# Routing batches of the last seven token tiles, the gate tiles, and the preparation of the output weights in a fused FFT and mixture-of-experts kernel

## The chip, the cores and the metric

One core of a Trainium2 chip. The metric is the device time of one execution in microseconds (us). A core has four compute engines with a queue of instructions each: TensorE (PE, matrix multiplication into PSUM banks), VectorE (DVE), ScalarE (ACT) and GpSimd (POOL). SyncE (SP) issues plain DMA transfers. POOL issues the indirect ones, those that gather or scatter rows by a list of indices. An instruction waits at the head of its engine's queue for semaphores, and everything behind it waits with it.

## What is computed

```python
X = np.fft.fft(np.fft.fft(x, axis=1), axis=2).real      # x: 8 x 3072 x 256
t = X.reshape(8 * 3072, 256)
h = np.maximum(np.maximum(t @ w1, t @ w2), t @ w3)       # 768 wide
x = h @ w_out                                            # 24576 tokens x 256
do = x @ w_skip > 0                                      # tokens that see an expert
e = argmax(x[do] @ w_gate)                               # one of 8 experts, F = 1024
y = softmax_gate * (np.maximum(x[do] @ e1[e], 0) @ e2[e])
out = x;  out[do] = x[do] + y
```

## The kernel before

The real part of the transform is symmetric, so the work is done on half spectra, and fp32 products are made of two or three fp32r products (a value's high part and the rest). Four phases follow each other.

1. The transform (`fft_phase`), with the weights of layer 1 (`prep_weights`) folded into the second transform.
2. The first expert network, on 25 tiles (`tiles`: 23 of 512 columns, then 256 and 264). `period(t)` works through 12 units of layer 1 of tile t: 6 blocks f of the hidden width, two halves i each. PE writes two banks "pa" and "pb" per unit (L484 to L488), DVE joins them (`even` L500, `minus` L503, `plus` L506, `peak` L514), ACT and POOL split the result into high part and rest (`ht`, L520 and L521). Between the units stand the pieces of layer 2 of tile t-1: `linear` (PE into bank pl, ACT copies to `lin` L553, POOL adds L556 and L558) and `rest` (PE pz L565, DVE zt L569). Tiles 0 and 1 are ordered by an automatic scheduler, the later ones as the code is written.
3. Routing, mixed into the same periods. The finished tokens of a batch of tiles (`BATCHES`) get scores, an expert and a place. `ship` stores tokens and copies ten gate columns into a tile `st` (ACT, L590). `finish` is a chain of small DVE steps (L598 to L624, with an ACT exponential L603). `place` counts the tokens ahead of each one (PE L634 and L636, then DVE up to the index list rI, L646). Then one `scatter` (POOL, L651) for each block of 128 tokens, 193 in all, writes token number and gate into the list `lst`, sorted by expert. `st` comes from a pool and is cleared on POOL (L921) at the first tile of a batch. The scatters wait in a Python list (`posted`), and `period` takes one out at each unit.
4. The second expert network, 256 tokens of one expert at a time. Three static steps, whose tokens are known early (from tile 18 on), stand in the program: `wide1` (PE, L785), `wide1_rest` (ACT, then DVE hs L789), `layer2_of` (PE pys, L798), `result` (DVE L802) and `place_rows` (POOL, L805). `table` (DVE, L841 to L876) works out for the remaining tokens which step takes which expert. It needs all counts and so the placing of the last tile. Its result `tab` lets SP load the first lists of tokens (ida, idn, idm) and the first weights (ws), and POOL gather the first tokens (Gd, L1139). Two dynamic loops follow.

Between tile 24 and the dynamic loops lies a tail. It holds layer 2 of tile 24, the routing of the last batches, all scatters not yet issued (`post`, with a tiny add `idle` on POOL between two of them), and the three static steps.

In phase 2, at tile 0, a generator (`prep_out`, L381 to L406) also prepares the output weights: for each block f a transposition (PE pT, ACT woT), a gate product (PE pg, ACT wof) and a product with w3 (PE pc), which collects in two of the five "pa"/"pb" banks.

## Time and profile before

| | |
|---|---|
| three timed runs | 1717.25, 1718.05, 1723.55 us (median 1718.05) |
| the profiled execution | 1719.05 us, of which the span of instructions is 1717.1 us |
| mean granted clock of PE | 0.977 of full speed |
| busy in the span | PE 1614.2 us (94%), DVE 1336.0 (78%), POOL 1121.5 (65%), ACT 739.0 (43%) |
| transform | up to about 178 us |
| tile 0 of the first network | PE from 188.15 us |
| layer 2 of tile 24 on PE (tail begins) | 1166.04 us |
| dynamic loops on PE begin | 1247.87 us |

All times within a trace count from the start of its span. What an engine waited for stands in brackets behind a row. Idle time counts only on an engine that sets the pace.

### The profile page before, as it was taken

To read this page: it belongs to the slowest core of one execution; us is meant where nothing else is said; L and a number is where in the kernel's file an instruction comes from. 1 tells how busy PE (TensorE), PEld (TensorE's weight loads), DVE (VectorE), ACT (ScalarE), POOL (GpSimd) and SP (SyncE) were. 2 spreads that over 40 slices of the span, in tenths; PEclk is the share of its full clock that TensorE was granted. 3 is DMA by queue.
4 is the path that set the end of the run, shared out by engine and by line. 5 is a ranking of instruction groups with operands and counts; after the bars stand their busy time and mean duration, and the time that the engine had idled before them with its cause. 6 is when DMAs were issued, how large, how long until landed. Compare 5 with 4: busy or idle time off the path is not lost. (4 is left out here: it accounts for less than half of the span.)

```text
span 1717.1 us, 33375 instructions
## 1 busy us (share of the span) xinstructions
PE 1614.2 (94%) x10837; PEld 1448.1 (84%) x10837; DVE 1336.0 (78%) x2288; ACT 739.0 (43%) x1437; POOL 1121.5 (65%) x1358
## 2 busy tenths in 40 slices
PE   6999699999999999999999999994799999999985
PEld 2565489989889989899898898984799999999975
DVE  7999488888788888888887878882477777777754
ACT  4555343333333333333333333331266666666654
POOL 2000355668878789789688788698456666676753
PEclk9999799999999999999999999997899999999998
DMA  8875420412211111111122111122266766766766
GB/s 324 306 281 205 151 61 32 129 44 48 59 44 44 44 44 44 50 50 44 57 44 59 47 44 41 42 51 71 69 218 223 229 218 220 231 220 220 232 197 214
DMA packets 109435, 212.47 MB, mean 124 GB/s; under 512 B 28107, under 2 KB 61292, under 8 KB 106228
## 3 DMA queue, kind: packets, MB, share of 16 engines
q1 hardware_dynamic: 94360, 188.65, 34.7%
q0 software_dynamic: 14112, 21.77, 4.1%
q8 instruction: 56, 0.92, 0.3%
q10 hardware_dynamic: 864, 0.79, 0.1%
q14 instruction: 43, 0.35, 0.1%
HBM read 157.82 MB, written 55.17 MB: 124 GB/s over the span
## 5 line engine op out<-in xcount | busy, mean ns | idle before, releaser
L565 PE MATMUL pz<-wo,ht 128*128 128x266 f32 x3474 | 484.2, 286 | 3.1 <-ACT lin L553 3.1
L565 PEld LDWEIGHTS pz<-wo,ht 128*128 128x128 f32 x3474 | 462.6, 189 | 21.7 <-ACT lin L553 3.4
L521 POOL TENSOR_TENSOR ht<-u,ht 128x512 fp32r<-128x512 f32 (+2 forms) x300 | 374.9, 1256 | 161.6 <-ACT ht L520 153.9
L520 ACT ACTIVATE ht<-u 128x512 fp32r<-128x512 f32 (+2 forms) x300 | 175.6, 610 | 308.8 <-DVE u L514 304.0
L651 POOL DMA_INDIRECT lst<-pair,rI x193 | 191.6, 993 | 35.4 <-issue 28.8
L785 PE MATMUL acc<-xd,wd 128*128 128x256 f32 x1632 | 193.6, 278 | 0.9 <-DVEq L1249 0.9
L785 PEld LDWEIGHTS acc<-xd,wd 128*128 128x128 f32 x1632 | 190.3, 188 | 1.2 <-issue 1.2
L829 DVE TENSOR_TENSOR wd<-ws,wd 128x1024 fp32r<-128x1024 f32 x150 | 177.6, 1225 | 16.2 <-issue 6.0
L828 ACT ACTIVATE wd<-ws 128x1024 fp32r<-128x1024 f32 x150 | 154.9, 1061 | 76.2 <-issue 46.5
L553 ACT ACTIVATE lin<-pl 128x266 f32<-128x266 f32 x194 | 75.0, 393 | 211.8 <-DVE zt L569 149.4
L500 DVE SCALAR_TENSOR_TENSOR u<-yb,wv,pa 128x512 f32<-128x512 f32 (+2 forms) x124 | 89.8, 724 | 93.2 <-PE pa L486 80.9
L484 PE MATMUL pa<-y,wt 128*128 128x512 f32 (+2 forms) x300 | 118.4, 395 | 13.3 <-DVE y L459 10.4
L503 DVE TENSOR_TENSOR pa<-r,pb 128x512 f32<-128x512 f32 (+2 forms) x150 | 100.4, 669 | 34.7 <-ACT r L498 32.6
L798 PE MATMUL pys<-wd,hs 128*128 128x256 f32 x960 | 125.5, 286 | 1.2 <-DVE hs L1196 0.9
L789 DVE SCALAR_TENSOR_TENSOR hs<-acc,hs 128x512 fp32r<-128x512 f32 x148 | 98.0, 687 | 29.0 <-ACT hs L786 24.3
L798 PEld LDWEIGHTS pys<-wd,hs 128*128 128x128 f32 x960 | 117.7, 190 | 2.3 <-DVE hs L1196 1.3
L786 ACT ACTIVATE hs<-acc 128x512 fp32r<-128x512 f32 x148 | 86.9, 599 | 75.5 <-PE acc L785 72.5
L484 PE MATMUL pb<-y,wt 128*128 128x512 f32 (+2 forms) x300 | 117.6, 392 | 0.0
L485 PE MATMUL pb<-y,wt 128*128 128x512 f32 (+2 forms) x300 | 117.3, 391 | 0.0
L485 PE MATMUL pa<-y,wt 128*128 128x512 f32 (+2 forms) x300 | 117.0, 390 | 0.0
L486 PE MATMUL pa<-y,wt 128*128 128x512 f32 (+2 forms) x300 | 116.7, 389 | 0.0
L486 PE MATMUL pb<-y,wt 128*128 128x512 f32 (+2 forms) x300 | 116.4, 388 | 0.0
(286 smaller groups left out, 3190.4 us busy)
## 6 DMA issues: line engine op xcount, KB each, us to landing
ws<-e SPq DMA_DIRECT2D x164, 512.0 KB
xt<-xf SPq DMA_DIRECT2D x24, 1024.0 KB
out<-zt SPq DMA_DIRECT2D x48, 512.0 KB
yr<-ysc SPq DMA_DIRECT2D x25, 512.0 KB
ysc<-ytc SPq DMA_DIRECT2D x8, 768.0 KB
yb<-yfsc SPq DMA_DIRECT2D x23, 256.0 KB
ysc<-yts SPq DMA_DIRECT2D x8, 672.0 KB
wr<-wm SPq DMA_DIRECT2D x6, 768.0 KB
```

The source lines that it names most:

```text
L484: nc.tensor.matmul(pt[:, :w], wt[f][:, g, 0, c], hi, start=True, stop=False)
L485: nc.tensor.matmul(pt[:, :w], wt[f][:, g, 0, c], lo, start=False, stop=False)
L486: nc.tensor.matmul(pt[:, :w], wt[f][:, g, 1, c], hi, start=False, stop=not whole)
L503: nc.vector.tensor_tensor(minus_to, r, pb[:, :w], ALU.subtract)
L520: nc.scalar.activation(ht[:, 0, :w], h[:, s, :w], AF.Copy)
L521: nc.gpsimd.tensor_tensor(ht[:, 1, :w], h[:, s, :w], bits(ht[:, 0, :w]), ALU.subtract)
L565: nc.tensor.matmul(pz[:, :SW], hs[s][f][:, g, c * P : c * P + P], wo[:, v, f], start=f == 0 and g == 0 and v == 0, stop=f == NC6 - 1 and g ...
L651: ins = nc.gpsimd.indirect_dma_start(out=lst[:, :], out_offset=bass.IndirectOffsetOnAxis(ap=ix[:, b : b + 1], axis=0), in_=pair[:, first + b],
L785: nc.tensor.matmul(ph[:, f % 2 * 256 : f % 2 * 256 + 256], lhs, rhs, start=n == 0, stop=n == 5)
L798: nc.tensor.matmul(py[:, :D], lhs, rhs, start=n == 0, stop=n == 23)
L828: nc.scalar.activation(hi, r, AF.Copy)
L829: nc.vector.tensor_tensor(lo, r, bits(hi), ALU.subtract)
```

## The change

- **Batches.** Before: seven batches of three tiles, then (21, 22), (23) and (24). Now: six of three, (18, 19), then every tile from 20 to 24 by itself. The index lists rI have four buffers and not two. From tile 20 on every third unit takes two scatters from the list, the second behind an `idle` add.
- **Gate tiles.** Two lasting tiles `st0` and `st1` are cleared once, and the batches take turns. L921 has gone from POOL's queue.
- **Layer 2 from tile 21 on.** The second ACT copy of `linear` is dropped, and DVE makes the additions straight from the PSUM bank, in POOL's place.
- **Output weights.** `prep_out` runs in three stages (`turn`, `gates`, `product`) that work on three neighbouring blocks at a time. Its sums and its one shared transposition bank lie in the three layer-2 banks ("pz"), no longer in "pa" and "pb".
- **Tail.** Seven and four steps of routing go ahead of the first two parts of the first static `wide1`, `table` comes right after them, and the first loads and the first gather of the dynamic steps are issued ahead of the results of static step 2. Gd has its own buffer.

```diff
-BATCHES = [(3 * k, 3 * k + 1, 3 * k + 2) for k in range(7)] + [(21, 22), (23,), (24,)]
+BATCHES = [(3 * k, 3 * k + 1, 3 * k + 2) for k in range(6)] + [(18, 19)] + [(t,) for t in range(20, 25)]
-F1, F2, F3 = 3, 5, 6
+F1, F2, F4 = 3, 5, (4, 7)
+TL = 21
+TP = 20
@@ prep_out
-    pc = [mp.tile([P, 512], F32, tag=tag, name="pc", bufs=n) for tag, n in (("pa", PA), ("pb", 5 - PA))]
-    for f in range(NC6):
-        wof, w3t = raw[f // 2][:, f % 2, 0], raw[f // 2][:, f % 2, 1]
-        wo = pool.tile([P, SW], F32, tag="ws", name="wof", bufs=2)
-        nc.scalar.activation(wo[:, :D], wof, AF.Copy)
-        wT = pool.tile([P, 2, P], F32, tag="ws", name="woT", bufs=2)
-        pt = mq.tile([P, 512], F32, tag="pz", name="pT")
...
+    *pc, pt = (mq.tile([P, 512], F32, tag="pz", name=nm) for nm in ("pc", "pc", "pT"))
+    def turn(f):
+        wof, _ = part(f)
+        ws[f] = pool.tile([P, 3, SW], F32, tag="ws", name="wof", bufs=2)
         for kt in range(2):
             nc.tensor.transpose(pt[:, kt * P : kt * P + P], wof[:, kt * P : kt * P + P], ident)
+        nc.scalar.activation(ws[f][:, 1, :D], pt[:, : 2 * P], AF.Copy)
+        nc.scalar.activation(ws[f][:, 0, :D], wof, AF.Copy)
+    def gates(f):
+        pg = pt[:, 2 * P : 2 * P + 10]
         for kt in range(2):
+            nc.tensor.matmul(pg, ws[f][:, 1, kt * P : kt * P + P], gs[:, kt], start=kt == 0, stop=kt == 1)
+        nc.scalar.activation(ws[f][:, 0, D:], pg, AF.Copy)
+    def product(f):
+        nc.scalar.activation(wo_t[:, 0, f], wo, AF.Copy)
         for g in range(2):
             nc.tensor.matmul(pc[g][:, :SW], w3t[:, g * P : g * P + P], wo, start=f == 0, stop=f == NC6 - 1)
         nc.gpsimd.tensor_tensor(wo_t[:, 1, f], wo, bits(wo_t[:, 0, f]), ALU.subtract)
+    for k in range(NC6 + 2):
+        for stage, f in ((gates, k - 1), (product, k - 2), (turn, k)):
+            if 0 <= f < NC6:
+                stage(f)
         yield
@@ linear
-                    nc.scalar.activation(lin[c][:, k], pl[:, :SW], AF.Copy)
+                    if k == 0 or t < TL:
+                        nc.scalar.activation(lin[c][:, k], pl[:, :SW], AF.Copy)
-                nc.gpsimd.tensor_tensor(lin[c][:, 2], lin[c][:, 0], lin[c][:, 1], ALU.add)
+                eng, odd = (nc.gpsimd, lin[c][:, 1]) if t < TL else (nc.vector, pl[:, :SW])
+                eng.tensor_tensor(lin[c][:, 2], lin[c][:, 0], odd, ALU.add)
@@ place
-            ix = mr.tile([P, KB], I32, tag="rI", name="rI")[:, :nb]
+            ix = mr.tile([P, KB], I32, tag="rI", name="rI", bufs=4)[:, :nb]
@@ arrive
-                stage["st"], stage["o"] = mr.tile([P, KB, 10], F32, tag="st", name="st"), 0
-                nc.gpsimd.memset(stage["st"][:, :, E1:], 1e-9)
+                stage["st"], stage["o"] = stage["sts"][k % 2], 0
@@ period
-                        if posted and (n < 9 or t + 1 < len(tiles)):
-                            posted.pop(0)()
-                if t == 0 and i == 1:
-                    for _ in range((0, 0, 1, 2, 2, 2)[f]):
-                        next(prep)
+                        for k in range(2 if t >= TP and n % 3 == 0 else 1):
+                            if posted and (n < 9 or t + 1 < len(tiles)):
+                                if k:
+                                    apart()
+                                posted.pop(0)()
+                if t == 0 and n >= 3:
+                    next(prep)
@@ tail
-            for _ in range(2):
-                fill()
-            for q in range(4):
+            for q in range(2):
+                for _ in range(F4[q]):
+                    fill()
                 wide1(x, w, h, q, ph[q])
-            for q in range(4):
-                for _ in range(F3):
-                    fill()
+            wide1_rest(h, 0, ph[0])
+            settle()
+            wide1_rest(h, 1, ph[1])
+            steps = table()
+            next(steps)
+            for q in range(2, 4):
+                wide1(x, w, h, q, ph[q])
+            for q in range(2, 4):
                 wide1_rest(h, q, ph[q])
-            settle()
```

**Order, PE at tile 0, in the middle of the output weights.** `pT` or `pg`, `pc` and `wof` belong to the preparation, `pa` and `pb` to layer 1. Before:

```order
L393 MATMUL pg<-gs,woT 128x10 x2
L389 MATMUL pT<-ident,wraw_1466 128x128 x2
L396 MATMUL pc<-wof,wraw_1466 128x266 x2
L484 MATMUL pb<-y_1358,wt_72 128x512
L485 MATMUL pb<-y_1358,wt_72 128x512
L486 MATMUL pb<-y_1358,wt_72 128x512
L393 MATMUL pg<-gs,woT 128x10 x2
```

Now, at the same unit (L498 to L500 are the old L484 to L486):

```order
L398 MATMUL pT<-gs,wof 128x10 x2
L406 MATMUL pc<-wof,wraw_1440 128x266 x2
L498 MATMUL pa<-y_1360,wt_72 128x512
L391 MATMUL pT<-ident,wraw_1442 128x128 x2
L499 MATMUL pa<-y_1360,wt_72 128x512
L500 MATMUL pa<-y_1360,wt_72 128x512
L498 MATMUL pb<-y_1360,wt_72 128x512
L499 MATMUL pb<-y_1360,wt_72 128x512
L500 MATMUL pb<-y_1360,wt_72 128x512
L398 MATMUL pT<-gs,wof 128x10 x2
```

The w3 product `pc` of a block used to stand one transposition behind the gate product of its own block. Now it stands a whole step, a unit of layer 1 or so, behind it.

**Order, POOL in the tail, from the scatters to the first dynamic gather.** `lst` scatters are those of the routing, `out<-Gs` those of static results. Before (of the tail's 34 scatters 29 stand ahead of the memset and five behind it):

```order
L651 DMA lst<-pair,rI 228480x2
L921 MEMSET st 128x24
L1032 TENSOR_TENSOR idle<-zz 128x2
L651 DMA lst<-pair,rI 228480x2
...
L805 DMA out<-Gs,ids_11716 27776x256
L1032 TENSOR_TENSOR idle<-zz 128x2
L1139 DMA Gd<-out,ida 128x256 x2
```

Now (all 16 scatters of the tail stand ahead of the results):

```order
L667 DMA lst<-pair,rI 228480x2
L751 TENSOR_TENSOR idle<-zz 128x2
L827 DMA out<-Gs,ids_11249 27776x256
L751 TENSOR_TENSOR idle<-zz 128x2
L827 DMA out<-Gs,ids_11249 27776x256
L751 TENSOR_TENSOR idle<-zz 128x2
L1137 DMA Gd<-out,ida 128x256 x2
L751 TENSOR_TENSOR idle<-zz 128x2
L827 DMA out<-Gs,ids_11260 27776x256
```

The memset has gone, 18 scatters have moved into the periods ahead, and the gather Gd stands ahead of the results of static step 2.

**Order, PE in the tail, from layer 2 of tile 24 on.** `pr` is the placing of tile 24, the `pc` product begins `table`, `pt` ends it. Before:

```order
L565 MATMUL pz<-wo,ht 128x266 x54
L785 MATMUL acc<-xs,wx 128x256 x48
L634 LDWEIGHTS tri
L634 MATMUL pr<-sl,tri 128x45
...
L798 MATMUL pys<-wx,hs 128x256 x24
L768 MATMUL acc<-ident,Gs 128x128 x4
L841 LDWEIGHTS ones
L841 MATMUL pc<-sl,ones 128x8
L798 MATMUL pys<-wx,hs 128x256 x24
L785 MATMUL acc<-xs,wx 128x256 x36
L875 MATMUL pt<-ident,r_12993 1x128 x2
```

Now:

```order
L581 MATMUL pz<-wo,ht 128x266 x54
L807 MATMUL acc<-xs,wx 128x256 x24
L650 LDWEIGHTS tri
L650 MATMUL pr<-sl,tri 128x45
...
L863 LDWEIGHTS ones
L863 MATMUL pc<-sl,ones 128x8
L807 MATMUL acc<-xs,wx 128x256 x24
L820 MATMUL pys<-wx,hs 128x256 x24
L897 MATMUL pt<-ident,r_12931 1x128 x2
L790 MATMUL acc<-ident,Gs 128x128 x4
```

The placing of tile 24 and the first product of `table` now stand between the two halves of the first `wide1`, and the end of `table` behind the first `layer2_of`.

## Rows read from the trace of the kernel before

**Rows 1.** Page, busy time of the engines over the span

```profile
PE 1614.2 (94%) x10837; PEld 1448.1 (84%) x10837; DVE 1336.0 (78%) x2288; ACT 739.0 (43%) x1437; POOL 1121.5 (65%) x1358
```

**Rows 2.** Windows: stretch, length, PE, PEld, DVE, ACT, POOL, PEclk, DMA share, GB/s

```profile
206.60:216.40 9.80, 9.64 (x27) 7.23 (x28) 3.10 (x5) 4.30 (x12) 7.85 (x7) 0.51 0.18 55
...
1110.00:1160.00 50.00, 46.67 (x380) 45.26 (x379) 38.97 (x112) 17.85 (x54) 44.42 (x55) 1.00 0.20 44
...
1172.80:1247.90 75.10, 41.98 (x312) 40.57 (x310) 24.14 (x65) 11.54 (x21) 46.87 (x78) 0.75 0.19 52
```

**Rows 3.** Timeline of PE in the tail: start, length, operation, wait in brackets

```profile
1172.82 5.81 PE L785 MATMUL acc<-xs,wx 128*128 128x256 f32 x48
1187.88 0.20 PE L634 MATMUL pr<-sl,tri 128*128 128x45 bf16 x1 [9.25 <-DVE sl L615]
...
1208.65 3.78 PE L798 MATMUL pys<-wx,hs 128*128 128x256 f32 x16 [18.24 <-DVE hs L789]
...
1221.64 2.89 PE L798 MATMUL pys<-wx,hs 128*128 128x256 f32 x24
1224.37 0.60 PE L768 MATMUL acc<-ident,Gs 128*128 128x128 f32 x4
...
1239.99 0.46 PE L768 MATMUL acc<-ident,Gd 128*128 128x128 f32 x2 [4.01 <-DMA Gd<-out,ida]
...
1247.87 2.30 PE L785 MATMUL acc<-xd,wd 128*128 128x256 f32 x16 [0.89 <-DVEq L1249]
```

**Rows 4.** Timeline of DVE in the tail

```profile
1181.35 0.17 DVE L646 CAST rI<-rs 128x4 int32<-128x4 f32 x1 [12.30 <-DMA lst<-pair,rI]
...
1184.80 0.20 DVE L598 TENSOR_REDUCE rm<-st 128x5 f32<-128x40 f32 x1 [0.28 <-ACT st L590]
...
1207.61 0.20 DVE L622 TENSOR_REDUCE rS<-st 128x5 f32<-128x45 f32 x1 [18.90 <-POOL st L921]
...
1214.45 0.16 DVE L843 TENSOR_TENSOR tf<-pc,kt 128x8 f32<-128x8 f32 x1
...
1218.29 0.15 DVE L871 TENSOR_SCALAR r<-r 128x1 f32<-128x1 f32 x1
```

**Rows 5.** Timeline of POOL in the tail

```profile
1207.42 0.15 POOL L921 MEMSET st<- 128x24 f32 x1
...
1211.03 0.99 POOL L651 DMA_INDIRECT lst<-pair,rI  x1 [3.33 <-DVE rI L646]
...
1216.55 0.99 POOL L651 DMA_INDIRECT lst<-pair,rI  x1 [0.16 <-issue]
...
1236.06 2.03 POOL L1139 DMA_INDIRECT Gd<-out,ida  x1 [6.24 <-issue]
```

**Rows 6.** Timeline of SP in the tail, the loads behind `tab`

```profile
1222.95 0.40 SPq L824 DMA_DIRECT2D ida<-lst  x1
```

**Rows 7.** Groups by line from 1060 to 1160 us: count, busy, mean ns

```profile
L651 POOL DMA_INDIRECT lst<-pair,rI x15 | 14.8, 990 | 2.4 <-issue 2.4
...
L556 POOL TENSOR_TENSOR lin<-lin 128x266 f32<-128x266 f32 x11 | 7.2, 659 | 0.1
```

**Rows 8.** The same view, DVE

```profile
L569 DVE TENSOR_TENSOR zt<-pz,lin 128x266 f32<-128x266 f32 x21 | 9.0, 429 | 0.6 <-issue 0.6
```

**Rows 9.** Timeline of PE at tile 0

```profile
206.68 2.14 PE L396 MATMUL pc<-wof,wraw 128*128 128x266 f32 x4 [2.81 <-ACT wof L394]
...
221.68 0.61 PE L393 MATMUL pg<-gs,woT 128*128 128x10 f32 x4 [0.61 <-ACT woT L390]
```

**Rows 10.** Timeline of ACT at tile 0

```profile
205.50 1.06 ACT L462 ACTIVATE y<-yr 128x1024 fp32r<-128x1024 f32 x1 [3.33 <-POOL yr L448]
```

**Rows 11.** Timeline of DVE at tile 0

```profile
214.94 0.75 DVE L500 SCALAR_TENSOR_TENSOR u<-yb,wv,pa 128x512 f32<-128x512 f32 x1 [6.66 <-PE pa L486]
...
223.38 0.75 DVE L500 SCALAR_TENSOR_TENSOR u<-yb,wv,pa 128x512 f32<-128x512 f32 x1 [2.49 <-PE pa L486]
...
234.97 0.68 DVE L514 SCALAR_TENSOR_TENSOR u<-u,pb 128x512 f32<-128x512 f32 x1
```

78 lines of the change are left out of this document (39 added, 39 removed).

## The prediction

> **What bounds the kernel now.** I read the page first. PE is busy for 94% of the span [rows 1], so the kernel is as fast as PE is kept fed, and what can be gained lies where PE stands. Windows show where that is. Inside the first network PE has next to no gaps. At tile 0 PE looks busy in 9.64 of 9.80 us, but the granted clock is 0.51, the 1.2 GHz level. In the tail PE is busy for 42 of 75.1 us, at a mean granted clock of 0.75 [rows 2]; more exactly it lasts 75.05 us, from the first `wide1` at 1172.82 to the dynamic loops at 1247.87 [rows 3].
>
> The timelines tell what PE stands for in the tail. It waits 9.25 us for `sl`, the last step of tile 24's routing that PE needs, then 18.24 us for `hs` [rows 3]. DVE explains both. It stood 12.30 us at the rI of tile 23, because that buffer was still read by a scatter; tile 24's outputs and routing were queued behind it. Then it stood 18.90 us at rS, waiting for the memset of `st`, and the `hs` that PE wanted was behind that [rows 4]. The memset lay on POOL at 1207.42, behind 29 scatters that follow one another every 1.38 us ((1216.55 - 1211.03) / 4) [rows 5]. So the chain is: scatters on POOL, memset, DVE, PE. `table` (1214.45 to 1218.44 on DVE [rows 4]), the load of ida (1222.95 [rows 6]) and the gather Gd (1236.06 [rows 5]) come after, and PE waits for Gd 4.01 us more [rows 3].
>
> **The tail.** With four rI buffers, the index list of tile 24 goes into that of tile 20, whose scatters are long done. With lasting gate tiles no memset stands behind scatters. Both DVE stalls lose their cause. What is left to PE is its own work, at full clock: three `wide1` of 48 matmuls (5.81 us each), six `layer2_of` of 24 (2.89 us each), three transpositions (0.60 us each) [rows 3], together 17.4 + 17.3 + 1.8 = 36.5 us, and about 1 us for placing and table products: 37.5.
>
> Then the new waits. All routing of tile 24 stands ahead of PE's third part of `wide1`. Layer 2 of tile 24 ends at 1172.82, and its last outputs on DVE a little later. From rm to the `sl` for PE took 3.1 us (1184.80 to 1187.88 [rows 3, 4]), so `sl` is ready at about 1176, when PE has just done the first half of `wide1` (2.9 us). PE places (0.4 us) and does the other half, to about 1179.2. DVE then has rI, two `hs` and the 4.0 us of `table` before it comes to the `hs` that `layer2_of` wants, at about 1181.5. I put 2.3 us for that, 0.9 for the loop's entry as before [rows 3], and 1 for small delays. So 37.5 + 4.2 = 41.7 us in place of 75.05: **33.4 us gained**.
>
> Is something else late? Of 34 scatters in the tail 16 remain, some 22 us from the start of the tail at 1166, to 1188. `tab` is ready at about 1185, so SP loads ida at about 1188, now behind the first weights. Before, Gd began 13.1 us after the load of ida (1222.95 to 1236.06 [rows 5, 6]). If it takes as long again, it begins at about 1201 and is there 4 us later (1236.06 to 1239.99 [rows 3, 5]), at 1205. PE needs it 4.4 us before the loop (a transposition, a `layer2_of` and the entry), at about 1210. It is covered by 5 us. The ends: 28 us if this chain or `table` sets the pace for some 5 us, 37 us if no new wait shows.
>
> **The last three tiles.** 18 scatters move into them. With the adds between, POOL gets 18 x 1.38 = 25 us more there at the most. It loses 25 additions in all, 20 of them inside the periods, at 0.66 us: 13 us [rows 7]. From 1110 to 1160 POOL is already busy for 44.42 of 50 us and PE only 46.67 [rows 2], so POOL can be full there for some microseconds. Full POOL means late `ht`, and PE's `pz` behind it. DVE gets the 20 additions, at the nearest row (zt, also from PSUM, 0.43 us [rows 8]) 8.6 us, and some 4 us for two more rounds of routing of 13 small steps. In the same stretch it is busy for 38.97 us of 50 [rows 2]; the half of those 12.6 us that falls into it brings it to 45. Both engines come close to PE's own pace without clearly passing it. I take a loss of 1.5 us; bounds are a gain of 1 (PE loses 3.3 of these 50 us today, and part of it can be waits that go) and a loss of 6 (POOL full, with half of its net 12 us turned into waits).
>
> A moved scatter ran beside an idle DVE in the tail and now runs beside a busy one. The 15 scatters between 1060 and 1160, beside a busy DVE, took 990 ns on average [rows 7], those of the tail 0.99 [rows 5]: no stretching. The Trainium skill, "SBUF — State Buffer", section "Who interferes with whom", says that VectorE and GpSimd share a pair of ports under an exclusive lock. By that rule each of the 18 scatters could stand behind one DVE operation of 0.43 us [rows 8], which makes POOL 8 us later, and at the same half the loss here would be 4 us more. The scatters' durations don't agree with it.
>
> **Tile 0.** Before, PE stood 2.81 us for `wof` [rows 9]. ACT had it ready to do, but stood itself at `y` of a later tile for 3.33 us [rows 10]. The clock then dropped, and `pc` held two of the five banks of layer 1, so DVE, which is the slowest here, ran dry: 6.66 and 2.49 us [rows 11]. From 208.28 (where the first of these waits begins) to the last `peak`'s end at 235.65 DVE has three blocks of eight operations of about 0.6 us, and two for `cc`: 15.6 us of work in 27.4. So 11.8 us is the most that can be gained. In three stages `pc` no longer waits for the `wof` just made, and layer 1 has all of its five banks. The `y` stays in ACT's queue, ahead of the next gate copy, but PE then has a unit of layer 1 to do, six matmuls: I let half of the 3.33 us come back, 1.7. The one transposition bank also ties PE to ACT once a step; over six steps I put 0.6 us each, as `pg` once waited for `woT` [rows 9], 3.6 in all. 11.8 - 1.7 - 3.6 gives **6.5 us gained**. Bounds: nothing (the waits take it all) and 11.
>
> **Costs at nothing.** The dropped ACT copies (ACT is busy for 43% [rows 1]) and `idle` adds in the periods are hidden behind PE.
>
> **Sum.** 1719.05 (this execution's own time, 1.0 above the median of the three runs) - 33.4 - 6.5 + 1.5 = 1680.7. The median of runs then is 1679.7; I say 1679.
>
> **Rivals.**
> - **The tail keeps half of its stall.** The chain of `table`, ida, Gd or the scatters is longer than I think: for example when Gd again waits for weights or results in flight. For it: 13.1 us passed from ida to Gd before, with nothing in between that the profile names (the bracket says "issue" [rows 5]). Against: it has 5 us to spare and no PE instruction waits for the scatters. If it lasts twice as long, 26 us, PE stands 8 us more; with `table` late too, 15. Time 1688 to 1695. Chance 0.13.
> - **POOL or DVE is the bound in the last tiles.** Loss of 6 to 10 us in place of 1.5: 1684 to 1688. For it: 44.42 of 50 us busy. Chance 0.14.
> - **Nothing from tile 0.** ACT and the single bank replace the waits, or the clock falls anyway: 1686. Chance 0.12.
> - **Slower than before.** The clock. PE's granted clock is 0.75 in the tail because it fell while PE stood. If PE's short waits are enough to keep it at 1.2 GHz, PE's 37.5 us in the tail become 75, with the waits 79 (+4). At tile 0 the 17.6 us of those 27.4 that lie outside the half-clock window take up to twice as long; I put half of that, 9 us. Time 1719 + 4 + 9 = 1732. It decides only from nine tenths of the tail's work at the low level on (37.5 x 1.9 + 4.2 = 75.5, the old time). Against: PE ran at 1.2 GHz only behind stalls of 2.81 us or more here [rows 2, 3, 9], and the one I expect is shorter. Chance 0.02. By the Trainium skill, "TensorE: Matmul & The Clock Gate", PE's clock follows its activity, which agrees with these rows.
>
> **Numbers.** My forecast has 0.55 (1672 to 1684); 0.04 is left for no change, where the moved scatters or `st` wait somewhere that I don't see and the tail's gain is lost. Range 1667 (tail 37, tile 0 11, median offset 1, and 3 of other small gains) to 1695 (half of the tail's stall kept, or two of the losses together). A change of less than 0.5%, 8.6 us, is about what a measurement of this kernel can't tell from none. Faster by more than that 0.94, within it 0.04, slower 0.02.
>
> **What would show it.** Right: no wait of DVE for `st` or for rI; PE from the first `wide1` to the loop in 40 to 44 us with a clock near 1.0; PE waiting some 2 us for `hs` behind `table`; Gd without a wait of PE; at tile 0 no stretch at half clock behind `pc`, and the first `pz` near 231 us and not 237.6. Wrong: a new wait of over 5 us in the tail (Gd, `tab`), `pz <- ht` or `pl <- lin` waits from 1060 us on, or a first `pz` after 235 us.

## The result

The changed kernel takes 1703.38 us (median of four runs, 1702.47 to 1704.85); the kernel before, run beside it, 1717.65 us (1714.57 to 1723.55). The ratio is 0.9914 with a 95% interval of 0.9886 to 0.9941: faster by 0.86%. The forecast was 1679 us, and 1703 lies above its range. The direction was right; of the 38.4 us forecast for the profiled execution 16.0 came (1719.05 to 1703.05).

The profile page of the changed kernel, busy time of the engines [rows 1]:

```profile
PE 1618.0 (95%) x10839; PEld 1452.9 (85%) x10839; DVE 1356.6 (80%) x2341; ACT 735.9 (43%) x1426; POOL 1115.1 (66%) x1321
```

PE is busy for 3.8 us more than before. A change that only takes waits away leaves PE's busy time alone or, with the clock back up, lowers it. So somewhere PE's own work has become slower. I divide the execution at three places on PE: the first `pz` (end of tile 0), the first static `wide1`, and the first dynamic step. Their starts in the changed kernel, in the timeline of PE:

```profile
231.36 1.86 PE L581 MATMUL pz<-wo,ht 128*128 128x266 f32 x13
...
1174.37 3.04 PE L807 MATMUL acc<-xs,wx 128*128 128x256 f32 x24
...
1180.38 1.58 PE L820 MATMUL pys<-wx,hs 128*128 128x256 f32 x12
1182.71 0.50 PE L820 MATMUL pys<-wx,hs 128*128 128x256 f32 x2 [0.75 <-issue]
1185.41 1.22 PE L820 MATMUL pys<-wx,hs 128*128 128x256 f32 x4 [2.20 <-DVE r L892]
1190.61 1.95 PE L820 MATMUL pys<-wx,hs 128*128 128x256 f32 x6 [3.98 <-ACT hs L808]
...
1193.49 3.98 PE L820 MATMUL pys<-wx,hs 128*128 128x256 f32 x24
...
1221.99 0.78 PE L807 MATMUL acc<-xd,wd 128*128 128x256 f32 x3 [0.88 <-DVEq L1273]
```

Before, the last two stood at 1172.82 and 1247.87 [rows 3], the span ended at 1717.1, and the first `pz` was

```profile
237.60 3.86 PE L565 MATMUL pz<-wo,ht 128*128 128x266 f32 x30
```

That gives a ledger (us, worked out from these starts and the ends of the spans):

```
                                 before    after   change  forecast
start to first pz (tile 0)       237.60   231.36    -6.2     -6.5
first pz to first wide1          935.22   943.01    +7.8     +1.5
first wide1 to dynamic loops      75.05    47.62   -27.4    -33.4
dynamic loops to the end         469.2    479.1     +9.9      0
sum                                                -16.0    -38.4
```

Three lines are off, and the largest miss is one that the prediction has no term for. The windows of the four places [rows 2] (columns: stretch, length, busy time and count of PE, PEld, DVE, ACT, POOL, granted clock, DMA share, GB/s):

```profile
206.60:216.40 9.80, 9.13 (x50) 7.79 (x51) 6.83 (x11) 6.93 (x20) 8.47 (x8) 1.00 0.17 55
1015.60:1061.83 46.23, 41.40 (x256) 36.27 (x254) 41.09 (x80) 13.93 (x30) 34.90 (x35) 1.00 0.13 38
1061.83:1174.37 112.54, 106.49 (x798) 100.56 (x799) 102.01 (x255) 33.35 (x85) 91.59 (x105) 0.98 0.24 63
...
1185.20:1195.40 10.20, 6.00 (x25) 5.31 (x26) 2.16 (x5) 1.20 (x2) 3.53 (x6) 0.50 0.03 4
1222.00:1701.00 479.00, 451.46 (x3748) 448.07 (x3748) 338.72 (x463) 302.22 (x436) 313.55 (x508) 0.98 0.67 217
```

The same stretches of before, from the last zt of tile 19 to that of tile 20, from there to the first `wide1`, and the loops, were:

```profile
1021.95:1060.85 38.90, 38.78 (x248) 35.22 (x247) 31.74 (x55) 13.29 (x27) 35.65 (x34) 1.00 0.16 48
1060.85:1172.82 111.97, 105.87 (x807) 100.28 (x806) 87.34 (x224) 37.91 (x97) 85.76 (x103) 1.00 0.22 61
...
1247.90:1717.00 469.10, 442.85 (x3748) 438.69 (x3748) 339.04 (x463) 301.06 (x436) 299.44 (x506) 0.98 0.69 221
```

**Tile 0**: 50 instructions of PE in the time of 27, and the clock at 1.00 in place of 0.51. **The middle**: up to the end of tile 19 the lead of 6.35 us from tile 0 is whole (1015.60 to 1021.95). It goes in one period, tile 20's, which takes 46.23 us in place of 38.90. There DVE has 80 instructions in place of 55, and is busy for 41.09 of 46.23 us. POOL has nearly the same count (35 and 34), but twice two of its scatters now follow each other with only an `idle` add between them, and PE, which waited for nothing here before, now waits twice for POOL's `ht`. Waits of PE from 1012 to 1066 us in the changed kernel (total, times, longest):

```profile
PE pz L581 <- POOL ht L535: 2.6, 2, 1.3
PE pa L498 <- DVE u L514: 1.7, 1, 1.7
```

From then on the two kernels take about as long (112.54 to 111.97), but not for the same work: the steps that choose the tokens of the static steps stood behind this point before and stand in tile 20's period now. **The tail**: PE waits 0.75 + 2.20 + 3.98 + 0.88 us, and for 10.2 us the granted clock is 0.50, the 1.2 GHz level. **The loops**: the same 3748 matmuls at the same mean clock take PE 8.6 us longer.

**The loops in detail.** One dynamic step on PE before (columns: start, length, operation):

```profile
1259.87 5.62 PE L785 MATMUL acc<-xd,wd 128*128 128x256 f32 x48
1265.33 0.60 PE L768 MATMUL acc<-ident,Gd 128*128 128x128 f32 x4
1265.68 3.07 PE L798 MATMUL pys<-wd,hs 128*128 128x256 f32 x24
```

and in the changed kernel:

```profile
1234.67 5.85 PE L807 MATMUL acc<-xd,wd 128*128 128x256 f32 x48
1240.36 0.60 PE L790 MATMUL acc<-ident,Gd 128*128 128x128 f32 x4
1240.71 3.09 PE L820 MATMUL pys<-wd,hs 128*128 128x256 f32 x24
```

`wide1` starts a matmul every 119 ns in place of 114 ((1240.36 - 1234.67) / 48 and (1265.33 - 1259.87) / 48), with no wait in it. The loops have 34 steps, so 33 distances from one step's start to the next. In the changed kernel none is below 11.82 us. Before, by the pitch of their matmuls, there were three paces: 20 steps at about 11.55 us like the one shown, 2 at 11.34, and 11 at about 11.75, in which `wide1` too went at 118 ns with its operands in the same place. One of these:

```profile
1317.61 5.82 PE L785 MATMUL acc<-xd,wd 128*128 128x256 f32 x48
```

At these paces the 33 distances make 382.9 us before and 390.1 now, 7.2 of the 9.9 us. Single longer steps make another 3.5 (4.1 us above these paces before, 7.6 now), and what follows the start of the last step is 0.8 us shorter. The longest step is the fifth, 14.38 us in place of 11.55: DVE stands 4.10 us for a scatter of results, and PE 1.42 us for `hs` behind it.

```profile
1273.24 0.48 DVE L824 SCALAR_TENSOR_TENSOR O<-pys,gt,Z 128x256 f32<-128x256 f32 x1 [4.10 <-DMA out<-O,idc]
...
1278.94 2.88 PE L820 MATMUL pys<-wd,hs 128*128 128x256 f32 x22 [1.42 <-DVE hs L811]
```

The diff has no line in the loops. But two more rI buffers of 96 bytes each move everything behind them in SBUF: `xd`, the moving operand of `wide1`, from byte 207808 of a partition to 208000.

**The late signals in the tail.** The timeline of ACT in the first static step:

```profile
1176.01 0.60 ACT L808 ACTIVATE hs<-acc 128x512 fp32r<-128x512 f32 x1
1177.61 0.60 ACT L808 ACTIVATE hs<-acc 128x512 fp32r<-128x512 f32 x1 [1.00 <-PE pc L863]
1182.06 0.60 ACT L808 ACTIVATE hs<-acc 128x512 fp32r<-128x512 f32 x1 [3.85 <-PE acc L807]
1189.96 0.60 ACT L808 ACTIVATE hs<-acc 128x512 fp32r<-128x512 f32 x1 [7.31 <-remote]
...
1198.94 0.60 ACT L808 ACTIVATE hs<-acc 128x512 fp32r<-128x512 f32 x1 [4.46 <-PE acc L807]
```

Each `hs` needs one part of `wide1`. By PE's records the four parts end at 1175.97, 1177.41, 1179.12 and 1180.54. The first two `hs` start 0.04 and 0.20 us later, the third and the fourth 2.94 and 9.42 us later. In the next two static steps it is 0.04 us for each. ACT has nothing else to do in between, and the profile names no releaser for the long one ("remote"). PE's last wait (3.98) follows from it. The wait of 2.20 ends on DVE, whose `hs` stands behind `table`:

```profile
1184.61 0.15 DVE L893 TENSOR_SCALAR r<-r 128x1 f32<-128x1 f32 x1
1184.68 0.68 DVE L811 SCALAR_TENSOR_TENSOR hs<-acc,hs 128x512 fp32r<-128x512 f32 x1
```

The granted clock falls at 1185.2, at the end of this wait and ahead of the last one.

### The profile page after: what moved, and what is told of

Its sections match the earlier page's. It is cut to its first block, busy times and chain, and to the rows that moved or that the text cites. A ratio compares the mean times of both kernels' runs of the same rounds, so it can differ in the third digit from the quotient of the medians.

```text
span 1701.1 us, 33464 instructions
## 1 busy us (share of the span) xinstructions
PE 1618.0 (95%) x10839; PEld 1452.9 (85%) x10839; DVE 1356.6 (80%) x2341; ACT 735.9 (43%) x1426; POOL 1115.1 (66%) x1321
## 5 line engine op out<-in xcount | busy, mean ns | idle before, releaser
L667 POOL DMA_INDIRECT lst<-pair,rI x193 | 190.5, 987 | 32.1 <-issue 27.4
L807 PE MATMUL acc<-xd,wd 128*128 128x256 f32 x1632 | 199.3, 281 | 0.9 <-DVEq L1273 0.9
L807 PEld LDWEIGHTS acc<-xd,wd 128*128 128x128 f32 x1632 | 196.1, 188 | 1.1 <-issue 1.1
L850 ACT ACTIVATE wd<-ws 128x1024 fp32r<-128x1024 f32 x150 | 154.9, 1060 | 73.1 <-PE pyd L820 53.8
L568 ACT ACTIVATE lin<-pl 128x266 f32<-128x266 f32 x181 | 69.9, 392 | 209.9 <-DVE zt L585 152.9
L498 PE MATMUL pa<-y,wt 128*128 128x512 f32 (+2 forms) x300 | 119.0, 397 | 14.1 <-DVE y L473 10.3
L517 DVE TENSOR_TENSOR pa<-r,pb 128x512 f32<-128x512 f32 (+2 forms) x150 | 100.0, 667 | 31.4 <-ACT r L512 27.4
L498 PE MATMUL pb<-y,wt 128*128 128x512 f32 (+2 forms) x300 | 117.2, 391 | 0.0
L500 PE MATMUL pa<-y,wt 128*128 128x512 f32 (+2 forms) x300 | 116.6, 389 | 0.0
L500 PE MATMUL pb<-y,wt 128*128 128x512 f32 (+2 forms) x300 | 116.1, 387 | 0.0
```

What stands on the lines that cost most here:

```text
L498: nc.tensor.matmul(pt[:, :w], wt[f][:, g, 0, c], hi, start=True, stop=False)
L500: nc.tensor.matmul(pt[:, :w], wt[f][:, g, 1, c], hi, start=False, stop=not whole)
L517: nc.vector.tensor_tensor(minus_to, r, pb[:, :w], ALU.subtract)
L667: ins = nc.gpsimd.indirect_dma_start(out=lst[:, :], out_offset=bass.IndirectOffsetOnAxis(ap=ix[:, b : b + 1], axis=0), in_=pair[:, first + b],
L807: nc.tensor.matmul(ph[:, f % 2 * 256 : f % 2 * 256 + 256], lhs, rhs, start=n == 0, stop=n == 5)
L850: nc.scalar.activation(hi, r, AF.Copy)
```

## The experiments

Theories at the start: for the loops, the address (A) against a disturbance that comes with the earlier start of the loops (B); for the middle, DVE is full in tile 20's period (D) against POOL with its doubled scatters (P); for the tail, the order of `table` on DVE (T) against late signals from elsewhere (S). "Middle", "tail" and "loops" below are the second to the fourth line of the ledger, from each run's profile; a lag is the time from the recorded end of a part of `wide1` to the start of its `hs` on ACT. Ratios are against the kernel before, with 95% intervals.

**1. The kernel before, with 192 bytes in front.**

```diff
+        pad = mr.tile([P, 48], F32, name="pad", bufs=1)
+        nc.gpsimd.memset(pad, 0)
```

> The kernel before with one thing added: a tile of 192 bytes per partition that nothing uses (cleared once on POOL), which moves the tiles behind it (xs, xd, hs and others) to the addresses that they have in the changed kernel. Theory A: the dynamic loops became 9.9 us longer in the changed kernel (469.2 to 479.1 us) because those addresses changed; then a wide1 of 48 matmuls, start of the first to start of what follows, goes from 5.46 to 5.69 us here as well, the loops take 479 us, and the time is 8 to 11 us above the kernel before. Rival: the loops are longer for another reason (Gd in its own buffer, the new order of the first loads); then wide1 stays at 5.46, the loops at 469 and the time within 3 us of before.

Ratio 1.0044 [1.0027, 1.0060], slower. Loops 477.0 us in place of 469.3, `wide1` 119 ns, 11.83 us for nearly every step. In the loops nothing but addresses has changed, so A holds for the pace. The fifth step is not longer here (11.83).

**2. The changed kernel at the addresses of before.** Two of the four rI buffers go into the last pool of SBUF.

```diff
-            ix = mr.tile([P, KB], I32, tag="rI", name="rI", bufs=4)[:, :nb]
+            state["rk"] = 1 - state.get("rk", 0)
+            ix = (mr, mw)[state["rk"]].tile([P, KB], I32, tag="rI", name="rI", bufs=2)[:, :nb]
```

> The changed kernel with two of its four rI buffers put into the last pool, so that xs, xd and hs stand at the addresses of before; nothing else differs. Theory A (addresses): wide1 of 48 at 5.46 us, loops at 469 us, time 1692 to 1695, some 9 to 10 us below the changed kernel. Rival (Gd, order of loads): loops at 479 us, time 1702 to 1705.

1696.71 us, ratio 0.9869 [0.9853, 0.9886]. Loops 472.3. The paces of before are back (23 steps at about 11.55 us, 8 at 11.75, 2 at 11.34), and the fifth step stays long (13.36). The address cost 6.7 us of time (1703.38 - 1696.71; 7.7 by the two ratios). Middle (944.8) and tail (47.2) are nearly as in the changed kernel. So the rest of the loops' growth, some 3 us of longer steps, isn't the address. It speaks for B, but no run isolates its cause.

**3. The additions of layer 2 back on POOL** (`TL = 99` in place of 21).

> The changed kernel with the layer-2 additions of the last tiles left on POOL, with both ACT copies. The changed kernel loses 7.9 us against before between the first pz of tile 0 and the first wide1. Theory B: DVE, at 97 to 100% in pieces of the last tiles, causes most of it; then the loss shrinks to 2 to 4 us and the time falls by 4 to 6 us. Rival: POOL is the scarcer engine (its queue takes 18 more scatters), and with the additions back on it the loss grows to 12 us or more, time up by 4 or more. Third: it is the routing's place (choose a tile earlier) and nothing changes beyond 2 us.

Ratio 0.9921 [0.9905, 0.9938]. The middle is 950.9, 7.9 us worse than the changed kernel's. The period of tile 20, which lies ahead of the switch, is the same in both (46.3). Its loss therefore isn't from the additions. From tile 21 on DVE is the better place for them: with the additions on POOL and ACT's second copy back, PE waits 5.7 us for ACT's `lin` and 3.9 for POOL's `ht`. The median, 1707.11 us, is only 3.7 above the changed kernel's, and the two intervals overlap.

**4. A seventh batch of three tiles** (18 to 20), then single tiles.

> The changed kernel with a seventh batch of three tiles (18, 19, 20) and single tiles from 21 on, so that choose and the first list loads come a tile later, as before. Theory C: the first 3.3 us of the loss appear in tile 20's period because choose stands there beside the doubled scatters; then they go, tiles 20 and 21 keep the 6.3 us lead, and the time falls by 3 to 5 us if the tail does not take it back. Rival B (DVE's added additions): the loss in tiles 21 to 24 stays, time within 2 us. Rival D: the scatters of tile 20 come later, the tail grows by up to 8 x 1.38 = 11 us of POOL, and the time rises.

Ratio 0.9956 [0.9939, 0.9972]. Tile 20's period falls to 42.2, but the tail grows to 57.6, with 28 scatters left from 1164 us on in place of 16. The split into small batches is worth its price. This run also separates the two engines in tile 20's period. DVE has no routing there and is as busy as before (31.96 us to 31.74), the doubled scatters remain, and the period is still 3.3 us longer than the 38.90 of before. The window, and PE's waits from 1012 to 1066 us:

```profile
1015.84:1058.01 42.17, 39.30 (x248) 35.32 (x247) 31.96 (x56) 13.13 (x27) 34.80 (x35) 1.00 0.14 42
PE pz L581 <- POOL ht L535: 2.7, 2, 1.5
```

That part of the loss is POOL's (P).

The loops take 471.6 us here at the changed kernel's addresses, with 11.82 us for most steps: fewer long steps and a shorter end. A total of the loops alone doesn't tell where the operands lie; the pace of the steps does.

**5. Experiment 2 with the counts of the static steps taken one batch later** (`EARLY = 20` in place of 18: with tile 20's batch, in the period where they stood before).

> The kernel of e2 (changed kernel, addresses of before), with choose and the tokens of the static steps taken at tile 20's batch and not at that of (18, 19). The period from tile 19's last zt to tile 20's last zt is 38.9 us before, 46.2 in the changed kernel and 46.2 in e2: nearly all of the loss in the middle. Theory C: it is choose, which now meets that period's routing and the doubled scatters on DVE and POOL; then that period falls to 39 to 42 us, part of it comes back a period later, and the time is 2 to 5 us below e2. Rival (the batch of two and the scatters alone): the period stays at 45 to 46 us, time within 2 us of e2.

Ratio 0.9867 [0.9844, 0.9890], as experiment 2. Tile 20's period falls to 42.9 us, and tile 21's takes back what it gained: the first `wide1` is at 1174.48. The choosing steps cost the time wherever they stand. With them in the same period as before, 4.0 us of the loss lie in tile 20's period (42.91 to 38.90) and 3.9 behind it (115.87 to 111.97).

**6. Experiment 2 with `table` behind all four `hs`.**

```diff
-            steps = table()
-            next(steps)
             for q in range(2, 4):
                 wide1(x, w, h, q, ph[q])
             for q in range(2, 4):
                 wide1_rest(h, q, ph[q])
+            steps = table()
+            next(steps)
```

> The kernel of e2 with table (4 us of DVE) behind the last two hs of static step 0, and not ahead of them; placing stays between the halves of wide1. The changed kernel has 6.9 us of waits of PE in the first layer2_of, and a clock of 0.5 for 10 us behind them. Theory T (DVE's order): the waits are table ahead of hs; then they shrink to under 1.5 us, the tail goes from 47.2 to 41 to 43 us and the time falls by 4 to 6. Rival S (signals): ACT starts the hs of parts 2 and 3 of wide1 2.9 and 9.4 us after PE's last matmul of that part, whatever DVE does; then ACT's delay stays, and the tail stays above 45 us.

Ratio 0.9889 [0.9864, 0.9914]. The tail is 50.7, longer by 3.4. ACT's third and fourth `hs` still start 6.8 and 9.8 us behind their matmuls, with `table` out of the way. T falls as the cause of the late signals.

**7. Experiment 2 with the placing and `table` behind all four parts of `wide1`.**

```diff
                 wide1(x, w, h, q, ph[q])
+            for q in range(2, 4):
+                wide1(x, w, h, q, ph[q])
             wide1_rest(h, 0, ph[0])
             settle()
-            wide1_rest(h, 1, ph[1])
+            for q in range(1, 4):
+                wide1_rest(h, q, ph[q])
             steps = table()
             next(steps)
-            for q in range(2, 4):
-                wide1(x, w, h, q, ph[q])
-            for q in range(2, 4):
-                wide1_rest(h, q, ph[q])
```

> The kernel of e2 with placing and table both behind all four parts of wide1, so that PE does 48 matmuls in one piece. Theory T: PE waits for the placing's DVE steps no longer, hs comes first, the tail is 41 to 44 us. Rival S2: the late start of ACT's hs comes from the small matmuls of placing and counting between the halves of wide1; then in this kernel each hs starts within 0.5 us of its matmuls, while in the kernel with table alone moved it is late still.

1695.52 us, ratio 0.9853 [0.9829, 0.9876]. The tail is 44.6, the lags 0.04, 0.36, 1.2 and 2.7 us: smaller, not gone.

**8. The kernel before with the new preparation of the output weights alone.**

> The kernel before with the new preparation of the output weights alone. If the stages of the kernel add up, the first pz of tile 0 comes 6.2 us earlier (231.4 and not 237.6), nothing else changes, and the time is 6 us (0.36%) below before. Rival: the lead is lost where the next stage waits for data (the first layer 2, or the tail's transfers), and the time is within 2 us of before.

Ratio 0.9958 [0.9941, 0.9975]. The first `pz` is at 231.30 and the first `wide1` at 1166.08, 6.7 us earlier than before. The gain of tile 0 is real, is kept through all 25 tiles, and doesn't cause the loss of the middle (934.8).

**9. Experiment 7 with the tail's scatters held in a list until the first `layer2_of` is written.**

```diff
+        held = [1]
-            while n and posted:
+            while n and posted and not held:
...
+            held.clear()
+            post(len(posted))
```

> The kernel of e7 with all scatters of the tail held back until the first layer2_of is issued, so that POOL issues none while PE works on the first wide1. In e7 ACT starts the four hs of static step 0 0.04, 0.36, 1.2 and 2.7 us after PE's last recorded matmul of the part; in the changed kernel 0.04, 0.2, 2.9 and 9.4; in steps 1 and 2, without scatters, 0.04 throughout. Theory S3: the scatters beside it make PE's finishing late; then all four are under 0.1 us here. Rival: it is something else about step 0 (its place behind the last layer 2, its weights); then they stay above 1 us in parts 2 and 3. The scatters end later here, so Gd can be late; the total, about 1695 to 1705, is not what this run is for.

One run, 1692.69 us; tail 41.9. It doesn't test what it was meant to: POOL isn't ordered against PE, and went on with the scatters from 1164.8, most of them at a pitch of 1.38 us, all the same. The lags were 1.04, 1.9, 0.98 and 0.05 us.

**10 and 11. Experiment 7 with the weights 64 bytes and `xd` 128 bytes further (xd at 207936), and with `xd` alone 64 bytes further (207872).**

> The kernel of e7 with 64 unused bytes ahead of the tiles of weights and 64 more ahead of xs and xd: the weights wd go from addresses that are multiples of 128 to 64 above one, xd goes from 207808 to 207936 (64 above a multiple of 128 in both), hs to a multiple of 128. Theory A2: a matmul of 256 columns takes 114 ns and not 118 when what streams through it begins 64 bytes above a multiple of 128; then wide1 stays at 5.46 us per 48 and layer2_of (weights stream) falls from 2.83 to 2.73 us per 24, the loops from 470 to 463 us, time 6 to 8 us below e7. Rival: only xd against another operand matters (or another modulus); then layer2_of stays at 2.83 to 2.93, or wide1 rises to 5.69.

> The kernel of e7 with 64 unused bytes ahead of xs and xd alone: xd goes from 207808 (64 above a multiple of 128) to 207872 (a multiple of 128); hs and the weights stay. Theory A2: wide1 of 48 rises from 5.46 to 5.69 us, layer2_of does not change, the loops are 8 us longer. Rival: the slow addresses of the changed kernel came from hs, or from xd against some other size; then wide1 stays at 5.46.

Ratio 0.9908 [0.9891, 0.9926], and one run of 1697.49 us. A step takes 11.85 and 11.84 us: slow in both. So `xd`'s address alone is enough to do it, and the rule of 64 above a multiple of 128 that I had made up is wrong.

**12. Experiment 7 without doubled scatters** (`TP = 99`).

> The kernel of e7 with one scatter per place in the list from tile 20 on, no doubled ones. Theory P: the doubled scatters fill POOL in tile 20's and 21's periods and cause part of the 7.3 us that the period of tile 20 lost; then that period falls from 46 to 42 us or less, and the tail grows, because more scatters are left for it (each 1.38 us), time above e7 by 2 to 8 us. Rival: DVE alone is full there, the period stays at 46 us.

Ratio 0.9870 [0.9854, 0.9887]. The middle is 2.7 us shorter, the tail 4.5 longer. The doubled scatters cost and give about the same in time. Their cost lies in tile 20's period, which falls from 46.28 to 43.05 us, and PE's waits for POOL's `ht` are gone there; what remains, from 1012 to 1066 us:

```profile
PE pa L498 <- DVE u L514: 2.0, 1, 2.0
```

DVE has its 80 instructions as in experiment 7. So P holds for about 3.2 of the 7.3 us, as in experiment 4, and D for the other 4.1.

**13. A map of the pitch by address.** 116 groups of 12 matmuls ahead of the first dynamic step of experiment 7, extra work on a buffer of zeros:

```diff
...
+            for sh, offs in ((0, range(0, 1025, 16)), (16, range(0, 257, 16)), ...):
+                for o in offs:
+                    for n in range(12):
+                        nc.tensor.matmul(pm[:, :256], w[n % 2][n // 2 % 2][:, n // 4 * P + sh : n // 4 * P + sh + P], xm[:, o : o + 256], start=n == 0, stop=n == 11)
```

> The version with placing and table behind all four parts (address 207808), and ahead of the first dynamic step, as extra work that nobody reads, 116 groups of 12 matmuls of 128x256 whose moving operand, 256 columns of zeros, starts at 207808 plus 0, 64, 128 and so on up to 4096 bytes; then the same up to 1024 bytes with the weights' slices 64, 128 and 192 bytes further. If the start address of the moving operand alone sets the pitch, the groups fall into two kinds, near 114 and near 120 ns, the slow ones among them at +64, +128 and +192, and the pattern comes back after some power of two of bytes. If it is the distance to the weights, the pattern moves with the weights' shift. If it is neither (a neighbour of the buffer or another engine's traffic), all groups have one pitch or a pitch that follows time and not address. The extra work is about 1392 x 0.117 = 163 us, so the execution takes about 1854 us.

One run, 1859.89 us with the extra work. The mean distance from start to start (ns) in each group, from the trace:

```
moving operand at 207808 +    0     64    128    192    256    320    384    448    512
weights as they were        114.2  118.4  118.2  118.6  115.4  118.4  118.1  118.7  115.4
weights + 64 bytes          118.2  116.1  118.4  118.1  118.6  115.4  118.4  118.2  118.6
weights + 128               117.8  117.8  113.3  118.4  118.1  118.7  115.4  118.4  118.1
weights + 192               119.3  118.2  118.6  115.4  118.4  118.1  118.7  115.4  118.4
```

The first line goes on like that up to + 4096: one address in four is fast. The fast ones move with the weights. These lie at multiples of 256 and 207808 is 192 above one, so a matmul is fast where the moving operand starts 192 bytes behind its weights modulo 256. The programs so far fit in one direction: at distances of 128 (after and experiment 1) and 0 (experiments 10 and 11) `wide1` is always slow. At 192 (before, experiments 2 and 7) it is fast in most steps, but before it was slow in 11 of 33.

**14. Experiment 7 with six small bf16 matmuls**, which wait for nothing, between the second and the third part.

```diff
+            pd = bank("pr")
+            for n, nm in enumerate(("tri", "ones", "ones", "ones", "ones", "ones")):
+                nc.tensor.matmul(pd[:, :45], kc[nm], kc["tri"][:, :45], start=n == 0, stop=n == 5)
```

> The version with placing and table behind all four parts, with six bf16 matmuls of 45 columns on constant tables, which wait for nothing and which nobody reads, between the second and the third part of the first wide1. There ScalarE began its four hs 0.04, 0.36, 1.2 and 2.7 us behind the recorded end of each part. If small bf16 matmuls between the halves hold up the completion signals, the third and fourth lag come back to 3 and 8 us or more, and the tail (44.6 us) grows by 3 to 5 us. If it isn't they, the lags stay at 1 to 3 us and the tail grows by the 1 us of the extra matmuls at most.

One run, 1698.11 us. Lags 0.04, 0.29, 1.6 and 2.5 us, tail 43.8: not the small matmuls.

**15. Experiment 2 with the tail's scatters left out** (`posted.pop(0)()` becomes `posted.pop(0)`; the tokens of 16 blocks keep padding in their lists).

> The changed kernel at the addresses of before, with the list scatters of the tail left out (their tokens stay at the padding rows, so some two thousand tokens get no expert's result; the idle adds stay). With them, ScalarE began the third and fourth hs of the first static step 3.7 and 9.5 us behind the recorded end of their matmuls, and the tail took 47.2 us. If the burst of scatters, one every 1.38 us, holds up the completion signals, the lags fall below 0.3 us, and the tail falls by 5 us or more, to 42 or less. If it doesn't, they stay at 2.7 to 4 and 8 to 9.6 us, and the tail falls by 2 us at most (from an earlier ida and Gd).

One run, 1692.75 us. The tail is 38.5 in place of 47.2. The timeline of ACT, to be set beside the one of the changed kernel above:

```profile
1177.73 0.60 ACT L809 ACTIVATE hs<-acc 128x512 fp32r<-128x512 f32 x1
1179.14 0.60 ACT L809 ACTIVATE hs<-acc 128x512 fp32r<-128x512 f32 x1 [0.81 <-PE acc L808]
1180.79 0.60 ACT L809 ACTIVATE hs<-acc 128x512 fp32r<-128x512 f32 x1 [1.05 <-PE acc L808]
1182.15 0.60 ACT L809 ACTIVATE hs<-acc 128x512 fp32r<-128x512 f32 x1 [0.76 <-PE acc L808]
```

All four lags are 0.04 us, with `table` where the changed kernel has it. Without the burst of scatters no signal is late. PE in the first `layer2_of`:

```profile
1185.95 1.45 PE L821 MATMUL pys<-wx,hs 128*128 128x256 f32 x10 [2.25 <-DVE hs L812]
```

The wait behind `table` is still there, 2.25 us, as large as in the changed kernel and as forecast (2.3). The granted clock stays at 1.00 through the tail.

**16. Experiment 7 with `layer2_of`'s operands 192 apart too.** One tile of 128 bytes moves from ahead of `hs` to ahead of `xd`.

```diff
+        cum0 = mx.tile([P, 32], F32, name="cum0", bufs=1)
+        nc.gpsimd.memset(cum0, 0.0)
...
-        cum = [mr.tile([P, 32], F32, name=f"cum{k}", bufs=1) for k in range(3)]
+        cum = [cum0] + [mr.tile([P, 32], F32, name=f"cum{k}", bufs=1) for k in (1, 2)]
```

> The version with placing and table behind all four parts, and one tile of 128 bytes moved from ahead of the activations to ahead of xd. xd stays at 207808; hs moves to 64 above a multiple of 256, so that the moving operand of layer2_of now also starts 192 bytes (modulo 256) behind its weights, as xd's does. If that distance sets the pitch, layer2_of of the loops falls from 119.4 (pys) and 117.5 ns (pyd) to 114 to 115, the loops lose 34 x 24 x (4.9 + 3.0) ns = 6.4 us (470.5 to about 464), and the time falls to about 1689. If the rule holds for wide1 alone, layer2_of stays above 117 and the time at 1695.

1694.58 us, ratio 0.9855 [0.9838, 0.9871], the time of experiment 7. PE in the dynamic steps, grouped by line, in experiment 7 (columns: count, busy us, mean ns, idle before):

```profile
L808 PE MATMUL acc<-xd,wd 128*128 128x256 f32 x1583 | 187.4, 278 | 0.0
L821 PE MATMUL pyd<-wd,hs 128*128 128x256 f32 x787 | 97.5, 279 | 0.0
```

and here:

```profile
L810 PE MATMUL acc<-xd,wd 128*128 128x256 f32 x1584 | 191.9, 281 | 0.9 <-DVEq L1275 0.9
L823 PE MATMUL pyd<-wd,hs 128*128 128x256 f32 x790 | 95.2, 277 | 0.0
```

From start to start, distances of over 200 ns left out, `layer2_of` falls from 118.6 (pys) and 117.1 ns (pyd) to 115.6 and 113.6, near the forecast. But `wide1` rises from 114.9 to 117.7 at an unchanged distance, and most steps still take 11.55 us. So the distance isn't the whole rule, and something that these runs don't name holds most steps at 11.55 us. The surprise lies in the tail. Its PE timeline:

```profile
1181.51 1.19 PE L823 MATMUL pys<-wx,hs 128*128 128x256 f32 x8
1183.37 2.09 PE L823 MATMUL pys<-wx,hs 128*128 128x256 f32 x16 [0.67 <-DVE hs L814]
1188.30 0.38 PE L900 MATMUL pt<-ident,r 128*1 128x128 f32 x2 [2.84 <-DVE r L895]
...
1215.94 6.07 PE L810 MATMUL acc<-xd,wd 128*128 128x256 f32 x48 [0.88 <-DVEq L1275]
```

It takes 40.3 us, and all lags are 0.04 us, though the burst is there. Its POOL timeline:

```profile
1178.16 0.99 POOL L670 DMA_INDIRECT lst<-pair,rI  x1 [0.16 <-DVE rv L628]
...
1179.54 0.98 POOL L670 DMA_INDIRECT lst<-pair,rI  x1 [0.16 <-issue]
```

So the burst is needed for the late signals and isn't enough. The only change is where some tiles lie; whether that acts by itself, or by shifting the scatters against the matmuls, isn't shown.

**17 and 18. Experiment 16 with two scatters at every second unit, and that with the list of experiment 9.**

```diff
-                        for k in range(2 if t >= TP and n % 3 == 0 else 1):
+                        for k in range(2 if t >= TP and n % 2 == 0 else 1):
```

> The run before, with two scatters at every second unit from tile 20 on in place of every third. If the burst of scatters holds up the completion signals, fewer of them in the tail make the lags and the tail shorter: 2 to 4 us less than the 44.6 of the same order before. If POOL and VectorE are full in the last tiles, the middle (943.4) grows by 1 to 3 us, and the two nearly cancel.

> The run before, and the scatters that are then left for the tail stand behind the first layer2_of in the order of the code. When that was done alone the tail fell by 2.7 us in the profile, though GpSimd went on with them early. If that gain is the burst's, the tail is another 1 to 3 us shorter than in the run before; if it was chance, the same.

Ratios 0.9882 [0.9854, 0.9910] and 0.9868 [0.9852, 0.9885]. The tails are 40.4 and 40.5 us, all lags again 0.04; the middle grows by 2.3 and 2.6 us. With the signals on time there was nothing left to gain from fewer scatters, only the price in the full periods. By their ratios experiments 7 and 16 are the best versions timed more than once, about 0.6% below the changed kernel.

## Why the prediction was wrong

The step that failed first is one that the sum doesn't have. It goes from the tail to the median and takes the dynamic loops as they were, since the diff doesn't touch them. They grew by 9.9 us in the profile. Shown for about 7 of these: the two added rI buffers move `xd` from a distance of 192 bytes to 128 (experiments 1, 2, 11 and 13), and undoing that alone gives back 6.7 us of time. The other 3 are single longer steps, which stay when the address is put back (experiment 2); their cause is open.

**"The last three tiles"** was mis-sized: +1.5 forecast, +7.8 measured, which is the second rival (6 to 10 us) and not the likeliest case. I took the load from 1110 to 1160 us. The loss of 7.3 us is 50 us earlier, in tile 20's period, where the counting for the static steps, the routing of a small batch and the first doubled scatters now meet. The 112.54 us behind it, in place of 111.97, look like a forecast come true, but the choosing steps have left that stretch; with them in it the loss there is 3.9 us (experiment 5). The mechanism that I named, POOL late with `ht` and PE's `pz` behind it, was there, for about 3.2 of the 7.3 us: it goes with the doubled scatters (experiment 12) and stays without any routing on DVE (experiment 4). The other 4.1 are the routing on DVE that now stands in this period; I had expected DVE to stay below PE's pace. Its 25 steps there take 11.9 us. Five of them, of 0.98 to 1.70 us and each beside one of POOL's splits (`ht` or `y`), make 6.9 of that. The moved additions, which I counted as a burden on DVE, took 7.9 us less in the middle than on POOL, and 3.7 us of time (experiment 3). The port rule weighed there (the Trainium skill, "SBUF — State Buffer", section "Who interferes with whom") didn't show in the scatters: all 193 took 987 ns on average on the page, 993 on the page of before.

**"The tail"** was right in its mechanism. DVE no longer waits for the memset of `st`, and for rI only 0.20 us, and Gd, whose gather begins at 1200.76, costs PE no wait. Mis-sized are the new waits, 4.2 us forecast and 0.75 + 2.20 + 3.98 + 0.88 = 7.8 measured, and PE's own work, 37.5 and 39.8. Of the waits the entry (0.88) and the one behind `table` (2.20) came as forecast (0.9 and 2.3). The 1 us "for small delays" is the term that failed: the other waits make 4.7, and they are gone with the late signals. Without the scatters beside it (experiment 15) the tail takes 38.5 us, with waits of 2.25 + 0.88 = 3.1 and 35.4 of work at full clock. So PE's work was forecast 2 us too long. Of the 4.4 us that it took more in the changed kernel, 0.7 goes with the addresses (39.08 in experiment 2) and the rest with the low clock. There the prediction's reason failed: it kept PE's clock up because PE had run at 1.2 GHz only behind stalls of 2.81 us or more. In the changed kernel it fell at the end of a wait of 2.20 us, 0.50 us of work behind one of 0.75. In experiments 15 and 16 waits of 2.25 and 2.84 us left it at 1.00. With the signals on time and another order of `table`, the tail takes 40.3 us (experiment 16); 41.7 was forecast.

**"Tile 0"** was right: 6.2 of 6.5 us, the first `pz` at 231.36 (forecast "near 231"), no half clock there [rows 2], and the single change in experiment 8 gives the same.

The four terms with their shown sizes make the time: -6.2 + 7.8 - 27.4 + 9.9 = -16.0. Three things stay open. One is why a burst of scatters and the place of some tiles together delay PE's completion signals. Another is what, at unchanged addresses, sets the pace of a dynamic step: why `wide1` goes at 114 ns in some steps and 118 in others, and most steps of experiment 16 stay at 11.55 us though `layer2_of` is faster. The third is what makes single steps of the loops longer.

## What to carry to other kernels

A change that adds a buffer moves the addresses of everything behind it: compare where the operands of the hot loops lie in both programs, and check one unchanged loop in the two traces first. Windows for the price of moved work must cover every period into which the order puts it, above all the one where several chains of small steps meet. Where two engines are nearly full there, runs that take the work of one away tell what each costs (here 3.2 us for POOL's, 4.1 for DVE's). Take experiments' effects one at a time: here a move by 192 bytes cost as much as the whole gain at tile 0.

## What the runs showed of the hardware

- The pitch of fp32r matmuls of 256 columns went from 114 to 118 or 119 ns with the distance, modulo 256 bytes, between the moving operand and the weights in SBUF; of four distances 64 bytes apart one was fast (experiment 13). In the loops that rule alone didn't settle the pitch of `wide1`: at the fast distance it went at 118 ns in 11 of 33 steps before, and in most steps of experiment 16.
- ACT began up to 9.8 us behind the recorded end of the matmuls that it needed (experiment 6), in the first static step; up to 1.13 us in the second, in experiment 4, where the scatters went on until 1206 us. It went away without the scatters beside it (experiment 15), and also with 128 bytes moved (experiment 16).
- A DVE step on 8 columns (`ru`, 128x8) took 1.70 us in the changed kernel, beside POOL's `ht`, and 0.23 before, where POOL was idle:

```profile
1022.26 1.70 DVE L712 TENSOR_SCALAR ru<-rc,rw 128x8 f32<-128x8 f32 x1
1022.65 1.27 POOL L535 TENSOR_TENSOR ht<-u,ht 128x512 fp32r<-128x512 f32 x1
...
1067.52 0.23 DVE L696 TENSOR_SCALAR ru<-rc,rw 128x8 f32<-128x8 f32 x1
```
